# A shorter weight conversion, four more split rows and a reordered plan in a channel-attention kernel

## The chip, the cores and the metric

The kernel runs on one core of a Trainium2 chip. The metric is device time in microseconds, taken as the median of a kernel's runs. The core has four engines that matter here: TensorE (PE, matmuls), VectorE (DVE), ScalarE (ACT) and GpSimd (POOL). SyncE (SP) issues nearly all DMAs. Each engine takes its instructions in the order in which they were written into its queue and waits at an instruction until what it needs is there.

## The reference

Two layers run one after the other on four batches of 6336 rows and 256 channels.

```python
qn = q / (norm(q, axis=1) + 1e-6);  kn = k / (norm(k, axis=1) + 1e-6)
s  = kn.T @ qn / tau                     # 256 x 256 per batch, a sum over 6336 rows
a  = softmax(s);  x = v @ a
gate = sigmoid(sum over 5 taps of conv_w[tap] * x shifted by tap rows)
out  = (gate * (x @ w_val)) @ w_out
```

`q`, `k` and `v` are 32-bit floats. The three weights come as 64-bit floats, because the reference scales them by a 64-bit number. Nothing of `x` is known before a whole batch of `q` and `k` has been summed into `s`, so each batch has two phases: a reduction over rows, then a pass over rows that makes the output.

## The kernel before

**Precision.** A float operand of a matmul is either taken whole (`raw`, 32-bit, slower) or as two halves: a high part rounded to the fast matmul type (ScalarE, line 435) and the rest (GpSimd, line 438). Three fast products, high x high, high x low and low x high, then stand in for one whole product. A "whole row" below is a block of 128 rows whose `q` and `k` go into the matmul as they are; a "split row" is one that goes in as halves.

**Reduction phase.** A batch has 49 blocks of 128 rows and one of 64, in 17 groups: group 0 has one block and the remainder, the others three blocks each. For a group, SyncE loads `q` and `k` (line 412) into one of seven `raw` buffers; ScalarE squares them (462); VectorE or GpSimd adds the squares to one of two running sums (466), whichever the plan picks; TensorE multiplies the rows into `s` (494). `nw` (lines 396 to 399) says how many of a group's blocks stay whole: all three in the first three groups and the last group of batch 0, two in its other groups, two in the first `NATIVE` groups of batch 1, none elsewhere. At the end of a batch the two running sums are added (554), column norms are made on TensorE (544), `s` is copied out of its accumulator (558), scaled, exponentiated, divided (600), transposed (613) and multiplied by `w_val` (626).

**Output phase.** Each batch is passed in 13 steps of 508 rows (the last 240). A step loads `v` (690), transposes (695), casts (699) and splits it (702), makes `x` and `x @ w_val` on TensorE (710), runs the taps mostly on VectorE (736), the sigmoid on ScalarE (747), the product (754), splits it (760, 763) and multiplies it by `w_out` (782), copies (791) and stores (796). The reduction groups of the next batch are put between the steps of this one, so that from the end of batch 0's reduction on both phases run side by side. In the late steps ("shared", `n > LAST_ROWS`) ScalarE and GpSimd take one of VectorE's taps (741, 744), and from a little later on every second step uses two accumulator banks that the reduction no longer needs.

**Weights.** `prepare_weights` turns a 64-bit float, held as a low and an upper 32-bit word, into a 32-bit high part and a low part. It does this with integer operations on VectorE, ten for `w_val` and `w_out` (128 x 512 elements each) and eleven for the small `conv_w`; each operation is a task of its own, so the plan can put other work between them. The scratch tile `f` lies in PSUM, the two words `lo` and `up` in SBUF.

**The plan.** The order of each engine's queue is not written out by hand. Every piece of work is a task with an engine, an estimated cost and its dependencies. `line` fixes a wanted order of TensorE's work; `deadlines` goes back from there and gives every task a due time; `WANTED` gives the weights' loads and conversions theirs. `run` then plays the tasks through in time: an engine takes the task that can start and has the earliest due time. A sum of squares may go to VectorE or GpSimd. A load may start no earlier than `AHEAD` us before it is due. A load is taken to land later by `LAG` (one value early, one late in the kernel, switching at 60 us). `SPREAD` says how many slots after its last group a batch's norms, (batch 0 only) spread, transposes and combine come in `line`. `LATE` sets how many steps ahead of the last batch the groups end. All these figures are the planner's own; they set an order and no time on the chip.

Of the kernel before, what the change touches and what calls it, by code (L numbers as in the profile page):

```python
# [8 lines left out]
F32 = mybir.dt.float32  # L9
# [4 lines left out]
ALU = mybir.AluOpType  # L14
# [2 lines left out]

P = 128
GROUP = 3
LEAD, NATIVE = 4, 4  # L20
VBUFS = 3
Q = 32
SIDE = 3
# [4 lines left out]
class Plan:  # L28
# [65 lines left out]
    def run(self, line):  # L94
        due = self.deadlines(line)
# [21 lines left out]
        dma_free, lanes, table = 0.0, [], "sqrt"  # L117
# [18 lines left out]
        while len(order) < len(T):  # L136
            best = None
            for e, keys in open_.items():
                c = [(r, key) for key in keys for r in [possible(key)] if r is not None]
                if not c:  # L140
                    continue
                now = max(free[e], min(r for r, _ in c))
                if best is None or now < best[0]:
                    best = (now, e, c)
            assert best, "nothing can start"
            now, e, c = best
# [8 lines left out]
            r, key = pick  # L155
            t = T[key]
            start = max(now, r)
            if isinstance(t["cost"], tuple):
                size, n, slow = t["cost"]
                for _ in range(n):  # L160
                    if len(lanes) >= 8:
                        start = max(start, lanes[-8])
                    free[e] = start + SLOT
                    dma_free = max(dma_free, start + SLOT + REACH) + size / n * slow / RATE
                    lanes.append(dma_free)
                    start = free[e]
                end = dma_free + HOP + (LAG[start > 60] if key[0] in "LV" else 0)
            else:
                free[e] = start + self.duration(t, e)
                if t["table"] and t["table"] != table:  # L170
                    table = t["table"]
                    free[e] += TABLE
                end = free[e] + (DRAIN if e == "PE" else HOP if e else 0)
# [33 lines left out]


START, HOP, DRAIN, SLOT, FLIGHT, REACH, RATE = 3.7, 0.12, 0.22, 0.45, 4.5, 1.6, 360000.0
LAG, RAWS = (0.8, 3), 7  # L210
PATIENCE, SLACK, AHEAD = 0.8, 1.5, 26
V_SLOW = 2.0
HEADS = True
NARROW, LATE = (0,), 5
SPREAD = ((0, 0, 0, 0), (3, 3, 3), (1, 2, 1), (0, 1, 0))
TABLE = 1.28
WANTED = {("load", "conv"): 28, ("load", "val"): 15, ("load", "out"): 40, ("ready", "out"): 60, ("ready", "conv"): 32, ("ready", "val"): 38}


@with_exitstack  # L220
def kernel(
# [13 lines left out]
    nc = tc.nc  # L235
# [81 lines left out]
    def prepare_weights(part):  # L317
# [4 lines left out]
        w = parts_w[part]  # L322
        n = w.shape[1]
        if WORDS == 2:
# [4 lines left out]
            yield  # L329
            nc.vector.scalar_tensor_tensor(lo, lo, 17, f, ALU.logical_shift_right, ALU.bitwise_or)  # L330
            yield
            nc.vector.tensor_scalar(f, up, 20, 0x7FF, ALU.logical_shift_right, ALU.bitwise_and)
            yield
            nc.vector.tensor_scalar(f, f, 896.0, 0.0, ALU.subtract, ALU.max)
            yield
            nc.vector.tensor_scalar(f, f, 255.0, 2.0 ** 23, ALU.min, ALU.mult)
            yield
            nc.vector.scalar_tensor_tensor(f, up, -0x80000000, f, ALU.bitwise_and, ALU.bitwise_or)
            yield
            nc.vector.scalar_tensor_tensor(w, lo, 2.0 ** -35, fs, ALU.mult, ALU.mult)  # L340
            yield
            nc.vector.tensor_scalar(f, f, 3, None, ALU.logical_shift_right)
            yield
            nc.vector.scalar_tensor_tensor(f, up, 0xFFE00, f, ALU.bitwise_and, ALU.bitwise_or)
            yield
            nc.vector.tensor_scalar(f, f, 3, None, ALU.logical_shift_left)
            w_high[part] = fs
            if part == "conv":
                yield
# [7 lines left out]
        if WORDS == 2:  # L357
            nc.scalar.copy(flat(halves_w[part][0]), w_high[part])

    PREP = {"val": 10, "conv": 11, "out": 10}  # L360

    def weight_tasks():

# [26 lines left out]
    def group_tasks(b, g):  # L390
# [3 lines left out]
        last = g == len(groups[b]) - 1  # L394
        nv = 2
        if b == 0:
            nw = GROUP if g < SIDE or last else 2
        else:
            nw = 2 if b == 1 and g < NATIVE else 0
        parts = [(P, 0, n)] + [(REST, n, 1)] * rest  # L400
# [557 lines left out]
```

## Time and profile before

| | us |
|---|---|
| runs shown: median (lowest to highest of 3) | 591.97 (591.7 to 593.29) |
| the profiled execution, its own time | 593.26 |
| its span, first to last instruction | 591.5 |
| TensorE busy | 585.7 |
| VectorE busy | 514.3 |
| GpSimd busy | 506.3 |
| ScalarE busy | 479.6 |

The profile is of one execution. A row of a timeline gives start and length in us from the start of the span, engine, source line, operation, the tile written and those read, their shapes, and how many instructions were merged into the row; a bracket at its end gives the idle time of the engine just before and what ended it. Matmuls overlap, so the length of one says little; the distance between starts says what TensorE needs. In a row of grouped instructions the figures behind the bar are busy us, mean ns of one, and idle time before them with what ended it. In the table by stage each engine has its busy time in the stretch, with the number of instructions in brackets, and then the granted TensorE clock, the busy share of the DMA engines and the GB/s moved. SPq and ACTq are the DMA issues on the queues of SyncE and ScalarE.

### The profile page before, as it was taken

To read this page: it belongs to the slowest core of one execution; us is meant where nothing else is said; L and a number is where in the kernel's file an instruction comes from. 1 tells how busy PE (TensorE), PEld (TensorE's weight loads), DVE (VectorE), ACT (ScalarE), POOL (GpSimd) and SP (SyncE) were. 2 spreads that over 40 slices of the span, in tenths; PEclk is the share of its full clock that TensorE was granted. 3 is DMA by queue.
4 is the path that set the end of the run, shared out by engine and by line. 5 is a ranking of instruction groups with operands and counts; after the bars stand their busy time and mean duration, and the time that the engine had idled before them with its cause. 6 is when DMAs were issued, how large, how long until landed. Compare 5 with 4: busy or idle time off the path is not lost.

```text
span 591.5 us, 10511 instructions
## 1 busy us (share of the span) xinstructions
PE 585.7 (99%) x3667; PEld 531.2 (90%) x3667; DVE 514.3 (87%) x792; ACT 479.6 (81%) x582; POOL 506.3 (86%) x241
## 2 busy tenths in 40 slices
PE   9999999999999999999999999999999999999997
PEld 8898899998989999998989998998998998888887
DVE  3996899999989899988788899988969989988774
ACT  6698989889899979787798989788559777767754
POOL 4997999999997999999887999999935778777743
PEclk9999999999999999999999999999999999999999
DMA  8999997958577797874766899678333464553214
GB/s 331 383 368 231 273 243 200 213 133 226 169 157 179 203 214 195 169 190 112 219 166 153 208 213 244 143 190 181 75 93 103 114 160 118 124 141 89 68 40 123
DMA packets 154943, 105.83 MB, mean 179 GB/s; under 512 B 111114, under 2 KB 137994, under 8 KB 154890
## 3 DMA queue, kind: packets, MB, share of 16 engines
q1 hardware_dynamic: 154467, 104.51, 68.7%
q8 instruction: 29, 0.48, 0.4%
q10 hardware_dynamic: 423, 0.65, 0.3%
q14 instruction: 24, 0.20, 0.1%
HBM read 79.18 MB, written 25.95 MB: 178 GB/s over the span
## 4 chain that ended last, share of the span: by engine, by line
PE 89%; DMA 6%; ACT 1%; POOL 1%; issue 1%; SPq 1%; DVE 0%; POOLq 0%; ACTq 0%
PE o_ps L782 24%; PE x_ps L710 23%; PE val_ps L710 23%; PE s_ps L494 17%; DMA raw<-in_q_dram 4%; PE o_ps L626 1%; DMA raw<-in_k_dram 1%; DMA v_raw<-in_v_dram 1%; ACT sq L462 1%; SPq L412 1%; PE o_ps L613 0%; POOL v_lo L702 0%; ACT hi L435 0%; POOL acc L466 0%; PE o_ps L546 0%
## 5 line engine op out<-in xcount | busy, mean ns | idle before, releaser
L736 DVE SCALAR_TENSOR_TENSOR gate<-x_ps,wa,gate 128x508 f32<-128x508 f32 (+1 forms) x400 | 271.2, 717 | 33.9 <-ACT gate L733 31.2
L438 POOL TENSOR_TENSOR lo<-raw,hi 128x1536 fp32r<-128x1536 f32 (+2 forms) x65 | 185.4, 2857 | 7.8 <-ACT hi L435 6.0
L702 POOL TENSOR_TENSOR v_lo<-v_raw,v_hi 128x1024 fp32r<-128x1024 f32 (+1 forms) x52 | 124.1, 2387 | 14.6 <-ACT v_hi L699 12.1
L763 POOL TENSOR_TENSOR g_lo<-gate,g_hi 128x1016 fp32r<-128x1016 f32 (+2 forms) x52 | 120.7, 2322 | 16.9 <-ACT g_hi L760 16.6
L466 DVE TENSOR_TENSOR acc_ps<-acc_ps,sq 128x512 f32<-128x512 f32 (+1 forms) x146 | 101.2, 693 | 21.0 <-ACT sq L462 17.1
L710 PE MATMUL x_ps<-v_hi,w 128*128 128x512 f32 (+2 forms) x416 | 110.1, 384 | 0.0
L710 PE MATMUL val_ps<-v_hi,w 128*128 128x508 f32 (+1 forms) x416 | 107.8, 380 | 0.0
L462 ACT ACTIVATE sq<-raw 128x1536 f32<-128x1536 f32 (+2 forms) x68 | 95.8, 1413 | 3.0 <-POOL acc L466 1.7
L435 ACT CAST hi<-raw 128x1536 fp32r<-128x1536 f32 (+2 forms) x65 | 78.9, 1216 | 19.8 <-PE s_ps L494 11.1
L710 PEld LDWEIGHTS val_ps<-v_hi,w 128*128 128x128 f32 x416 | 76.1, 188 | 14.9
L710 PEld LDWEIGHTS x_ps<-v_hi,w 128*128 128x128 f32 x416 | 72.9, 188 | 12.8 <-POOL w L607 0.4
L733 ACT ACTIVATE gate<-x_ps,wa 128x508 f32<-128x508 f32 (+1 forms) x104 | 68.5, 664 | 14.0 <-PE x_ps L710 13.7
L782 PE MATMUL o_ps<-wo_hi,g_hi 128*127 128x256 f32 (+1 forms) x396 | 79.3, 282 | 0.0
L782 PE MATMUL o_ps<-wo_lo,g_hi 128*127 128x256 f32 (+1 forms) x396 | 79.0, 281 | 0.0
L494 PE MATMUL s_ps<-lo,hi 128*128 128x256 f32 x310 | 78.5, 287 | 0.0
L494 PE MATMUL s_ps<-hi,lo 128*128 128x256 f32 x310 | 77.2, 283 | 0.0
L791 ACT COPY o_sb<-o_ps 127x512 f32<-127x512 f32 (+1 forms) x99 | 57.8, 587 | 23.5 <-PE o_ps L782 23.1
L754 DVE TENSOR_TENSOR gate<-val_ps,gate 128x508 f32<-128x508 f32 (+1 forms) x104 | 67.4, 655 | 4.3 <-ACT gate L747 3.1
L699 ACT CAST v_hi<-v_raw 128x1024 fp32r<-128x1024 f32 (+1 forms) x52 | 57.5, 1107 | 16.0 <-PE val_ps L710 16.0
L466 POOL TENSOR_TENSOR acc<-acc,sq 128x512 f32<-128x512 f32 x46 | 59.9, 1301 | 10.9 <-ACT sq L462 9.6
L747 ACT ACTIVATE gate<-gate 128x1016 f32<-128x1016 f32 (+1 forms) x52 | 53.2, 1022 | 16.2 <-DVE gate L736 15.9
L782 PEld LDWEIGHTS o_ps<-wo_hi,g_hi 128*127 128x127 f32 (+1 forms) x396 | 62.7, 187 | 2.6
(96 smaller groups left out, 948.7 us busy)
## 6 DMA issues: line engine op xcount, KB each, us to landing
raw<-in_q_dram SPq DMA_DIRECT2D x64, 384.0 KB, 5.9
v_raw<-in_v_dram SPq DMA_DIRECT2D x192, 128.0 KB, 5.3
raw<-in_k_dram SPq DMA_DIRECT2D x63, 384.0 KB, 6.2
out_dram<-o_sb SPq DMA_DIRECT2D x47, 448.0 KB, 3.2
out_dram<-o_sb SPq DMA_DIRECT2D x47, 60.0 KB, 3.0
v_raw<-in_v_dram SPq DMA_DIRECT2D x16, 64.0 KB, 2.4
out_dram<-o_sb SPq DMA_DIRECT2D x3, 240.0 KB, 2.7
raw<-in_q_dram SPq DMA_DIRECT2D x4, 128.0 KB, 4.0
```

The costliest lines, as they stand in the source:

```text
L435: nc.scalar.copy(t["hi"][r, js], t["raw"][r, js, :, :])
L438: nc.gpsimd.tensor_tensor(t["lo"][r, js], t["raw"][r, js, :, :], t["hi"][r, js].bitcast(F32), ALU.subtract)
L462: nc.scalar.activation(t["sq"][0:np_, ja:jb], t["raw"][0:np_, ja:jb], AF.Square)
L466: eng.tensor_tensor(st[key][0:np_], st[key][0:np_], t["sq"][0:np_, j], ALU.add)
L494: nc.tensor.matmul(st["s"][:, h, :], lhs, rhs, start="open" not in st, stop=stop)
L702: nc.gpsimd.tensor_tensor(t["vl"][:, :, 0:g, :], t["v"], t["vh"][:, :, 0:g, :].bitcast(F32), ALU.subtract)
L710: nc.tensor.matmul(dst, weights[b][:, which, ws, ch, hs], vs[:, ch, at + lo:at + hi_], start=n_ == 0, stop=n_ == len(ops) - 1)
L733: nc.scalar.activation(t["gate"][:, h, 0:w], t["x", h][:, 0:w], AF.Copy, scale=cw[:, h, 0:1])
L736: nc.vector.scalar_tensor_tensor(t["gate"][:, h, 0:w], t["x", h][:, k_:k_ + w], cw[:, h, k_:k_ + 1], t["gate"][:, h, 0:w], ALU.mult, ALU.add)
L754: nc.vector.tensor_tensor(t["gate"][:, h, 0:w], t["val", h][:, 0:w], t["gate"][:, h, 0:w], ALU.mult)
L763: eng.tensor_tensor(t["gl"][:, hs, 0:w], t["gate"][:, hs, 0:w], t["gh"][:, hs, 0:w].bitcast(F32), ALU.subtract)
L782: nc.tensor.matmul(t["o", p][0:rows, u * C:(u + 1) * C], gs[:, h, j * rows:(j + 1) * rows], ws[:, h, :], start=(u, n_) == (0, 0) if HEADS ...
```

## The change

It has four parts.

- **Conversion.** The exponent and the top 11 bits of the fraction are now taken out of `up` together (shift by 9, mask of 22 bits), and the two clamps run on this longer number. That makes the high part at once; three operations that put the fraction in afterwards fall away. One new operation masks the sign and exponent out of the result into `up`, and the low part is the product of `lo` and `up`, both in SBUF, where it was the product of `lo` and the scratch tile in PSUM. Eight operations are left for the large weights and nine for the small one.
- **Rows.** In groups 3, 6, 9 and 12 of batch 0 (`EASED`) one block stays whole and two are split; it was two and one. `NATIVE` goes from 4 to 5: in group 4 of batch 1 two blocks of three stay whole, where none did.
- **Planner's figures.** `LAG` is now (0.8, 2.5), switching at 30 us (`LAG_AT`); `AHEAD` is 18 for 26; the weights' due times in `WANTED` are changed; and GpSimd may take a sum of squares no earlier than `SPARE` = 100 us before it is due.
- **Order.** `SPREAD` is changed for batches 1 to 3; `LATE` is 4 for 5, so the last group comes one step later, and the shared steps and those with the two extra banks begin one step later.

```diff
-LEAD, NATIVE = 4, 4
+LEAD, NATIVE = 4, 5
...
-                c = [(r, key) for key in keys for r in [possible(key)] if r is not None]
+                c = [(max(r, due[key] - SPARE) if e == "POOL" and key[0] == "A" else r, key) for key in keys for r in [possible(key)] if r is not None]
...
-                end = dma_free + HOP + (LAG[start > 60] if key[0] in "LV" else 0)
+                end = dma_free + HOP + (LAG[start > LAG_AT] if key[0] in "LV" else 0)
...
-LAG, RAWS = (0.8, 3), 7
-PATIENCE, SLACK, AHEAD = 0.8, 1.5, 26
+LAG, RAWS = (0.8, 2.5), 7
+PATIENCE, SLACK, AHEAD = 0.8, 1.5, 18
...
-NARROW, LATE = (0,), 5
-SPREAD = ((0, 0, 0, 0), (3, 3, 3), (1, 2, 1), (0, 1, 0))
+NARROW, LATE = (0,), 4
+SPREAD = ((0, 0, 0, 0), (2, 1, 1), (2, 1, 2), (2, 0, 0))
+SPARE, LAG_AT = 100, 30
+EASED = (3, 6, 9, 12)
...
-WANTED = {("load", "conv"): 28, ("load", "val"): 15, ("load", "out"): 40, ("ready", "out"): 60, ("ready", "conv"): 32, ("ready", "val"): 38}
+WANTED = {("load", "conv"): 28, ("load", "val"): 17, ("load", "out"): 36, ("ready", "out"): 56, ("ready", "conv"): 36, ("ready", "val"): 42}
...
-            nc.vector.tensor_scalar(f, up, 20, 0x7FF, ALU.logical_shift_right, ALU.bitwise_and)
+            nc.vector.tensor_scalar(f, up, 9, 0x3FFFFF, ALU.logical_shift_right, ALU.bitwise_and)
             yield
-            nc.vector.tensor_scalar(f, f, 896.0, 0.0, ALU.subtract, ALU.max)
+            nc.vector.tensor_scalar(f, f, 896.0 * 2 ** 11, 0.0, ALU.subtract, ALU.max)
             yield
-            nc.vector.tensor_scalar(f, f, 255.0, 2.0 ** 23, ALU.min, ALU.mult)
+            nc.vector.tensor_scalar(f, f, 255.0 * 2 ** 11, 2.0 ** 12, ALU.min, ALU.mult)
             yield
             nc.vector.scalar_tensor_tensor(f, up, -0x80000000, f, ALU.bitwise_and, ALU.bitwise_or)
             yield
-            nc.vector.scalar_tensor_tensor(w, lo, 2.0 ** -35, fs, ALU.mult, ALU.mult)
+            nc.vector.tensor_scalar(up, f, -0x800000, None, ALU.bitwise_and)
             yield
-            nc.vector.tensor_scalar(f, f, 3, None, ALU.logical_shift_right)
-            yield
-            nc.vector.scalar_tensor_tensor(f, up, 0xFFE00, f, ALU.bitwise_and, ALU.bitwise_or)
-            yield
-            nc.vector.tensor_scalar(f, f, 3, None, ALU.logical_shift_left)
+            nc.vector.scalar_tensor_tensor(w, lo, 2.0 ** -35, up.bitcast(F32), ALU.mult, ALU.mult)
...
-    PREP = {"val": 10, "conv": 11, "out": 10}
+    PREP = {"val": 8, "conv": 9, "out": 8}
...
-            nw = GROUP if g < SIDE or last else 2
+            nw = GROUP if g < SIDE or last else 1 if g in EASED else 2
```

## The prediction

> **What bounds the kernel now.** I read the page's busy shares first, then the table by stage, then what TensorE waited for, and last the instructions in order of time around each wait.
>
> ```profile
> span 591.5 us, 10511 instructions
> PE 585.7 (99%) x3667; PEld 531.2 (90%) x3667; DVE 514.3 (87%) x792; ACT 479.6 (81%) x582; POOL 506.3 (86%) x241
> ```
> ```profile
> core 0: us, PE busy (x) PEld busy (x) DVE busy (x) ACT busy (x) POOL busy (x), PEclk, DMA share, GB/s
> 24.00:36.00 12.00, 11.66 (x66) 10.57 (x65) 11.35 (x22) 10.71 (x12) 11.20 (x10) 1.00 1.03 402
> 36.00:49.00 13.00, 13.00 (x75) 12.07 (x73) 12.20 (x20) 11.21 (x14) 12.47 (x11) 1.00 1.01 285
> 49.00:62.00 13.00, 12.64 (x74) 10.84 (x73) 6.87 (x16) 10.80 (x18) 9.81 (x8) 1.00 1.00 271
> 62.00:160.00 98.00, 98.00 (x620) 88.86 (x619) 95.90 (x140) 87.34 (x95) 97.92 (x39) 1.00 0.83 202
> ...
> 430.00:490.00 60.00, 60.00 (x375) 53.82 (x374) 50.12 (x79) 44.87 (x68) 36.62 (x20) 1.00 0.49 124
> ...
> 60.00:570.00 510.00, 510.00 (x3231) 1.00 0.68 165
> ```
> ```profile
> PE o_ps L613 <- ACT a L600: 0.4, 1, 0.4
> PE s_ps L494 <- DMA raw<-in_k_dram: 0.3, 1, 0.3
> ```
>
> TensorE is busy 510.00 of the 510 us between 60 and 570, at the full clock. Behind the start it waits twice, 0.3 and 0.4 us (0.34 and 0.36 in the rows further down). The end is short too:
>
> ```profile
> 587.25 0.40 PE L782 MATMUL x_ps<-wo_hi,g_lo 128*120 128x256 f32 x2
> ...
> 588.13 0.35 SPq L803 DMA_DIRECT2D out_dram<-o_end  x1
> ```
>
> From the last matmul's end (587.65) to the end of the span are 3.9 us of copy and store, which no part of the change touches. So the time can move in two ways only: by the work given to TensorE, and by waits of TensorE that close or open. The other engines count when they are late for it. GpSimd and VectorE have little room: 97.92 and 95.90 of 98 us in the stage from 62 to 160, 12.47 and 12.20 of 13 from 36 to 49.
>
> **TensorE's own work.** A group of three rows costs by its mix of whole rows (fp32, four instructions each) and split rows (high and low halves, six each):
>
> ```profile
> 35.49 1.89 PE L494 MATMUL s_ps<-raw 128*128 128x256 f32 x8
> ...
> 37.94 1.89 PE L494 MATMUL s_ps<-raw 128*128 128x256 f32 x8
> ```
> ```profile
> 84.80 2.16 PE s_ps L494 x18
> ```
>
> Two whole rows and one split row take 37.94 - 35.49 = 2.45 us; three split rows take 2.16, so 0.72 each. A whole row is (2.45 - 0.72) / 2 = 0.865, that is 0.145 more. The change turns one whole row into a split one in groups 3, 6, 9 and 12 of batch 0: -4 x 0.145 = -0.58 us. `NATIVE` = 5 leaves two rows of group 4 of batch 1 whole: +2 x 0.145 = +0.29. Net -0.29 us. As TensorE is full, this is gained outright if nothing else is late.
>
> **The waits in batch 0.**
>
> ```profile
> 25.17 2.00 PE L494 MATMUL s_ps<-raw 128*128 128x256 f32 x8 [0.34 <-DMA raw<-in_k_dram]
> ...
> 26.82 0.59 PE L494 MATMUL s_ps<-hi 128*128 128x256 f32 x2
> 27.25 0.36 PE L494 MATMUL s_ps<-lo,hi 128*128 128x256 f32 x1
> ...
> 29.35 0.59 PE L494 MATMUL s_ps<-hi 128*128 128x256 f32 x2
> 29.93 0.39 PE L494 MATMUL s_ps<-lo,hi 128*128 128x256 f32 x1
> ```
> ```profile
> 13.22 1.15 SPq L314 DMA_DIRECT2D w_raw<-in_moe_w_out_dram  x1
> ...
> 17.67 0.33 SPq L412 DMA_DIRECT2D raw<-in_k_dram  x1
> ```
>
> Group 8's keys come 0.34 us late, and the low half of the next group comes late behind them: 29.93 - 29.35 is 0.58 where 27.25 - 26.82 is 0.43, so 0.15 more. The 512 KB of w_out stand at 13.22 in SyncE's queue, ahead of groups 7 and 8 (17.67 is group 8's k). Their load is due at 40 now and issued up to `AHEAD` = 26 us early, from 14 on in the planner's own clock; with 36 and 18 it is opened at 18, behind those groups, and a landing 10 us later is covered, as the first out product needs batch 0's softmax, which has reached only its division at 58 (below). At the 402 GB/s of that stage 0.52 MB are 1.3 us, more than the 0.34 needed, even after the 2 x 0.145 by which groups 3 and 6 let TensorE arrive earlier (0.34 + 0.29 = 0.63). w_val's load (due 15, now 17) steps behind group 6 in the same way. Term: -0.34 - 0.15 = -0.49; the bounds are -0.49 and, with loads as late as now and TensorE earlier, +0.58 (the whole saving of batch 0 spent waiting). I take the first, since 1.3 is twice 0.63.
>
> **What the other engines pay.**
>
> ```profile
> L438 POOL TENSOR_TENSOR lo<-raw,hi 128x512 fp32r<-128x512 f32 x18 | 23.1, 1288 | 1.0 <-ACT hi L435 1.0
> L702 POOL TENSOR_TENSOR v_lo<-v_raw,v_hi 128x1024 fp32r<-128x1024 f32 x48 | 118.9, 2476 | 14.3 <-ACT v_hi L699 11.8 <-DMA v_raw<-in_v_dram 2.4
> L466 DVE TENSOR_TENSOR acc_ps<-acc_ps,sq 128x512 f32<-128x512 f32 x142 | 98.4, 693 | 20.3 <-ACT sq L462 16.4
> L342 DVE TENSOR_SCALAR w_ps<-w_ps 128x512 int32<-128x512 int32 x2 | 1.4, 685 | 0.0
> ```
>
> Four second rows cost GpSimd 4 x (2.476 - 1.288) = 4.75 us in batch 0. Two conversion operations less for w_val and w_out save VectorE 4 x 0.685 = 2.74 (those of the ten-column conv weights come on top). The square sums may run on either engine: four sums moved from GpSimd, which takes 1.29 for any two-input operation of this shape, to VectorE give GpSimd 5.2 and cost VectorE 4 x 0.693 = 2.77. So both come out even; VectorE has 0.8 us spare from 36 to 49 besides. ScalarE's four longer casts (1.47 for three rows further down, so at most 0.49 for one more, 2.0 in all) fit in its idle 1.8 us from 36 to 49 and 1.3 from 24 to 36. I take 0 for all this, because the sums are dealt by due time to whichever engine is free. If none moved, GpSimd would be 4.75 late where its margin is small:
>
> ```profile
> 42.24 1.31 POOL L438 TENSOR_TENSOR lo<-raw,hi 128x512 fp32r<-128x512 f32 x1
> ...
> 44.80 0.28 PE L494 MATMUL s_ps<-lo,hi 128*128 128x256 f32 x1
> ```
>
> The low half ends at 43.55 and is used at 44.80: 1.25 us. So TensorE would wait 4.75 - 1.25 = 3.5. In batch 1 `NATIVE` takes two rows off a full GpSimd, about 2.4 us, so no debt is carried on.
>
> The new last conversion step reads both words from SBUF, where the old one read one from PSUM. No row here shows VectorE with two SBUF inputs beside GpSimd. Between 0 and one VectorE step for w_val and w_out each, 2 x 0.685 = 1.4 us of GpSimd, I take 0, as the margin above covers one. The Trainium skill ("SBUF — State Buffer", Who interferes with whom) says that such an instruction takes the read port of GpSimd, and the later of the two is blocked for the whole of the other. By that rule GpSimd loses the 1.4; no run here shows it yet.
>
> **The softmax of batch 0.**
>
> ```profile
> 46.18 0.69 DVE L554 TENSOR_TENSOR acc_all<-acc_ps,acc 128x512 f32<-128x512 f32 x1 [0.29 <-POOL acc L466]
> 48.13 0.59 ACT L558 COPY s<-s_ps 128x512 f32<-128x512 f32 x1
> 48.97 0.97 PE L544 MATMUL o_ps<-ones,acc_all 128*128 128x1 f32 x8
> ...
> 56.70 1.47 ACT L435 CAST hi<-raw 128x1536 fp32r<-128x1536 f32 x1 [1.04 <-POOL v_lo L702]
> 58.08 0.90 ACT L600 ACTIVATE a<-s,rz 128x256 f32<-128x256 f32 x2
> 58.64 0.84 PE L613 MATMUL o_ps<-ident,a 128*128 128x128 f32 x4 [0.36 <-ACT a L600]
> ```
>
> The norms follow the copy of s, which follows batch 0's last row, so this chain starts earlier by what batch 0 gains (its sums are done 1.3 us before the copy). Its one wait, 0.36, comes from a cast that stands ahead of the division on ScalarE and itself waits 1.04 us. The longer load time from 30 us on (`LAG_AT`) may reorder those two. Bounds -0.36 and +1.04 (the same stall twice on the path); I take 0.
>
> **What moves without a price.** `LATE` = 4 lets the groups run one step longer, and one shared step fewer moves 0.7 us from ScalarE and 1.3 from GpSimd to VectorE (0.7), in a stage (430 to 490) where VectorE is 50 of 60 us busy. Batch 3's softmax starts about a step later, some 10 us (the 527 us from 60 to the last matmul over 52 steps). It has that room: from its last row products to the first use of its weights are
>
> ```profile
> 442.69 1.44 PE s_ps L494 x12
> ...
> 478.02 0.62 PE L710 MATMUL x_ps<-v_hi,w 128*128 128x508 f32 x2
> ```
>
> 34 us, and batch 0's softmax took 9.7 from norms to transposes. `SPARE` = 100 bars GpSimd from a sum more than 100 us before it is due; with seven raw buffers none is loaded so early. `SPREAD` moves norms, transposes and combines by one to five slots in the order; TensorE takes the earliest due that can start, so I take 0, between -0.29 and +0.7 for each of three softmaxes: the one is what is lost at such a border now, the other two waits of batch 0's size.
>
> ```profile
> 307.44 0.84 PE L494 MATMUL s_ps<-hi 128*128 128x256 f32 x4
> 308.21 0.39 PE L494 MATMUL s_ps<-lo,hi 128*128 128x256 f32 x1
> ```
>
> Here four instructions take 0.77, where four of 0.72 / 6 = 0.12 take 0.48.
>
> **The sum.** -0.58 + 0.29 - 0.49 = -0.78 us. The profiled execution took 593.26 (span 591.5 and 1.76 around it), so 592.5 of its like; it lies 1.29 above the median of the runs, 591.97, which gives 591.2.
>
> **The rivals.**
>
> - The loads bind batch 0 anyway (1.03 of the DMA engines are busy there): TensorE's 0.58 turns into waiting and only `NATIVE` is left: 591.97 + 0.29 = 592.3. Against it speaks w_out's step back.
> - The waits close everywhere: -0.78, the 0.36, and three times 0.29 at the later softmaxes: -2.0, 590.0. It needs every reordering to hit.
> - Slower: GpSimd becomes the bound of batch 0, as its four longer subtractions stay in front of TensorE and the sums do not move: +3.5 less the 0.29 net saving, 595.2. It decides from the point at which no more than one of the four sums moves: at one, GpSimd is 4.75 - 1.29 - 1.25 = 2.2 late (593.9), at two 0.9 (592.6).
> - The port: 1.4 us of GpSimd fall on TensorE in place of none: 591.2 + 1.4 = 592.6. The skill's rule named above would make this one; the margin of 1.25 speaks against it.
> - Loads opened 18 and not 26 us ahead come late in the later stages. The longest landing up to 60 us (the last figure here) was 9.4 us and the due time already holds a flight of 4.5, so this needs a second cause; waits as long as batch 0's three together (0.34 + 0.36 + 1.04) give 591.2 + 1.7 = 592.9.
>
> ```profile
> DMA to landing us min/median/max: 2.7/6.9/9.4
> ```
>
> **How the numbers follow.** Forecast 0.50 (its own range 590.6 to 591.8), loads bind 0.16, all waits close 0.12, GpSimd binds 0.09, port 0.07, late loads 0.06. A measurement of this kernel tells about 0.3%, 1.8 us, from no change. Faster than 590.2 are most of the all-close case and the edge of the forecast: 0.12. Slower than 593.8 is GpSimd's case and a little of the late loads: 0.10. Within: 0.78. The range 590.0 to 592.9 leaves out GpSimd's case, half of the late loads and part of the fastest.
>
> **What would show it.** Right: eight raw matmuls fewer and twelve split ones more; w_out's load behind group 8's; no wait on a DMA at group 8; the sums of batch 0 with four fewer on GpSimd; norms about 1 us before 48.97; TensorE still full from 60 to 570. Wrong: TensorE waiting for a low half (L438) or raw in the stage 24 to 49, a GpSimd operation beside the new conversion step that is longer than 1.3 us, or new waits at the softmaxes of batches 1 to 3.

## The result and the profile after

The changed kernel takes 597.21 us (median of four executions, 597.12 to 598.37); the kernel before, timed beside it, takes 591.84 (591.62 to 593.29). The ratio is 1.009, with a 95% interval of 1.0078 to 1.0102. The change makes the kernel 5.4 us slower, where 0.8 us less was forecast. The profiled execution took 597.12 us.

The head of the page of the kernel after:

```profile
span 595.3 us, 10546 instructions
PE 587.1 (99%) x3671; PEld 532.0 (89%) x3671; DVE 517.9 (87%) x788; ACT 479.3 (81%) x581; POOL 506.8 (85%) x239
```

TensorE has four matmuls more (eight whole ones fewer, twelve of split rows more), as counted beforehand. The loss is found in the table by stage of the same kernel (the columns are named in its first line):

```profile
core 0: us, PE busy (x) PEld busy (x) DVE busy (x) ACT busy (x) POOL busy (x), PEclk, DMA share, GB/s
24.00:36.00 12.00, 11.73 (x70) 10.67 (x69) 10.98 (x22) 11.13 (x12) 9.76 (x7) 1.00 1.03 404
36.00:49.00 13.00, 12.21 (x69) 10.97 (x67) 12.44 (x18) 8.88 (x11) 9.33 (x8) 1.00 1.10 296
49.00:62.00 13.00, 12.19 (x62) 10.96 (x62) 12.55 (x20) 9.17 (x18) 7.78 (x6) 0.87 1.15 280
62.00:160.00 98.00, 96.72 (x607) 87.14 (x607) 93.74 (x137) 87.12 (x95) 96.56 (x40) 1.00 0.81 181
...
160.00:570.00 410.00, 410.00 (x2602) 371.68 (x2601) 360.29 (x543) 333.04 (x411) 359.23 (x161) 1.00 0.65 159
```

From 160 to 570 TensorE is full, as before. What is lost is lost ahead of 66 us (from 62 to 66 TensorE is busy for 2.72 of 4 us, from 66 to 160 for all 94): from 49 to 62 it starts 62 matmuls where the kernel before started 74, and its clock is 0.87. GpSimd, taken beforehand for the engine that could become late, is less busy there than before (9.33 for 12.47 us from 36 to 49, 7.78 for 9.81 from 49 to 62). VectorE is the fuller one from 49 to 62: 12.55 us for 6.87, and 4.10 of the 12.55 are one operation that comes below.

The view of what TensorE waited for, kernel after (total us, times, longest):

```profile
PE o_ps L542 <- DVE acc_all L552: 1.6, 1, 1.6
...
PE o_ps L624 <- ACT at_hi L615: 1.1, 1, 1.1
PE s_ps L492 <- DMA raw<-in_k_dram: 0.2, 1, 0.2
```

The two new waits are for the sums of batch 0 (line 552) and for its transposed weights (line 615), both parts of the softmax of batch 0; the 0.2 us for keys lie at 5.70, at the start. The same two places on TensorE's timeline, with the first matmul that uses the weights (line 708), which started at 60.04 before:

```profile
49.81 1.08 PE L542 MATMUL o_ps<-ones,acc_all 128*128 128x1 f32 x8 [1.60 <-DVE acc_all L552]
...
63.14 0.74 PE L624 MATMUL o_ps<-wv_hi,at_hi 128*128 128x256 f32 x4 [1.10 <-ACT at_hi L615]
...
64.66 0.62 PE L708 MATMUL x_ps<-v_hi,w 128*128 128x508 f32 x2
```

Why they are late is on VectorE's timeline. Line 344 is the new last step of the conversion, the one with both inputs in SBUF; `wa` are the conv weights, `wv_lo` and `wo_lo` the low parts of w_val and w_out; line 552 adds the two running sums; line 580 is the softmax's scale:

```profile
28.34 0.72 DVE L344 SCALAR_TENSOR_TENSOR wa<-w_raw 128x10 f32<-128x10 int32 x1
...
38.70 1.71 DVE L344 SCALAR_TENSOR_TENSOR wv_lo<-w_raw 128x512 fp32r<-128x512 int32 x1
...
49.06 0.69 DVE L552 TENSOR_TENSOR acc_all<-acc_ps,acc 128x512 f32<-128x512 f32 x1
...
51.87 4.10 DVE L344 SCALAR_TENSOR_TENSOR wo_lo<-w_raw 128x512 fp32r<-128x512 int32 x1
...
56.50 0.86 DVE L580 SCALAR_TENSOR_TENSOR s<-s,nk,o_ps 128x256 f32<-128x256 f32 x2
```

An operation of this shape took 0.685 us before. Here w_val's step takes 1.71 and w_out's 4.10, and even the ten columns of the conv weights take 0.72. GpSimd beside the two long ones:

```profile
39.82 1.73 POOL L464 TENSOR_TENSOR acc<-acc,sq 128x512 f32<-128x512 f32 x1
...
51.69 1.28 POOL L464 TENSOR_TENSOR acc<-acc,sq 64x512 f32<-64x512 f32 x1 [1.21 <-ACT acc L455]
52.92 1.27 POOL L436 TENSOR_TENSOR lo<-raw,hi 128x512 fp32r<-128x512 f32 x1
54.15 1.27 POOL L464 TENSOR_TENSOR acc<-acc,sq 128x512 f32<-128x512 f32 x1
55.63 1.48 POOL L464 TENSOR_TENSOR acc<-acc,sq 128x512 f32<-128x512 f32 x1 [0.20 <-ACT sq L460]
```

w_out's step starts 0.18 us after a GpSimd operation did. Three GpSimd operations then keep their length, 1.27 or 1.28. GpSimd has nothing to do from 55.42 to 55.63; w_out's step ends at 55.97, and the GpSimd operation behind that pause takes 1.48. w_val's step got in at the next change of operations: it ends at 40.41, and the GpSimd operation that started at 39.82 takes 1.73 in place of 1.29.

### The profile page after: what moved, and what is told of

Its sections match the earlier page's. It is cut to its first block, busy times and chain, and to the rows that moved or that the text cites. A ratio compares the mean times of both kernels' runs of the same rounds, so it can differ in the third digit from the quotient of the medians.

```text
span 595.3 us, 10546 instructions
## 1 busy us (share of the span) xinstructions
PE 587.1 (99%) x3671; PEld 532.0 (89%) x3671; DVE 517.9 (87%) x788; ACT 479.3 (81%) x581; POOL 506.8 (85%) x239
## 4 chain that ended last, share of the span: by engine, by line
PE 89%; DVE 5%; issue 2%; DMA 2%; ACT 2%; POOL 1%; SPq 0%; DVEq 0%; ACTq 0%; POOLq 0%
PE o_ps L780 24%; PE x_ps L708 23%; PE val_ps L708 23%; PE s_ps L492 17%; DVE acc_ps L464 3%; DMA raw<-in_k_dram 2%; ACT sq L460 1%; PE o_ps L624 1%; POOL lo L436 0%; ACT hi L433 0%; PE o_ps L542 0%; POOL acc L464 0%; DVE wv_lo L344 0%; PE o_ps L544 0%; PE o_ps L611 0%
## 5 line engine op out<-in xcount | busy, mean ns | idle before, releaser
L436 POOL TENSOR_TENSOR lo<-raw,hi 128x1536 fp32r<-128x1536 f32 (+3 forms) x65 | 186.4, 2874 | 10.9 <-ACT hi L433 10.8
L433 ACT CAST hi<-raw 128x1536 fp32r<-128x1536 f32 (+3 forms) x65 | 79.5, 1227 | 7.0 <-DMA raw<-in_k_dram 4.1
L464 POOL TENSOR_TENSOR acc<-acc,sq 128x512 f32<-128x512 f32 (+1 forms) x45 | 58.8, 1306 | 9.2 <-ACT sq L460 7.3
L780 PE MATMUL o_ps<-wo_hi,g_lo 128*127 128x256 f32 (+1 forms) x396 | 63.3, 282 | 0.0
```

The source lines that it names most:

```text
L433: nc.scalar.copy(t["hi"][r, js], t["raw"][r, js, :, :])
L436: nc.gpsimd.tensor_tensor(t["lo"][r, js], t["raw"][r, js, :, :], t["hi"][r, js].bitcast(F32), ALU.subtract)
L464: eng.tensor_tensor(st[key][0:np_], st[key][0:np_], t["sq"][0:np_, j], ALU.add)
L780: nc.tensor.matmul(t["o", p][0:rows, u * C:(u + 1) * C], gs[:, h, j * rows:(j + 1) * rows], ws[:, h, :], start=(u, n_) == (0, 0) if HEADS ...
```

## The experiments

Two theories stood at the start: the new last step loses time to GpSimd, since both its inputs are in SBUF (the port); or the new figures of the planner and the rows give a worse order (the order).

**The changed kernel without the second SBUF input (a_psum).** The three steps swap their scratch tiles, so that the eight operations stay and the last one reads one input from PSUM. The order of the work stays the same.

```diff
-            nc.vector.scalar_tensor_tensor(f, up, -0x80000000, f, ALU.bitwise_and, ALU.bitwise_or)
+            nc.vector.scalar_tensor_tensor(up, up, -0x80000000, f, ALU.bitwise_and, ALU.bitwise_or)
...
-            nc.vector.tensor_scalar(up, f, -0x800000, None, ALU.bitwise_and)
+            nc.vector.tensor_scalar(f, up, -0x800000, None, ALU.bitwise_and)
...
-            nc.vector.scalar_tensor_tensor(w, lo, 2.0 ** -35, up.bitcast(F32), ALU.mult, ALU.mult)
-            w_high[part] = fs
+            nc.vector.scalar_tensor_tensor(fs if part == "conv" else w, lo, 2.0 ** -35, fs, ALU.mult, ALU.mult)
+            w_high[part] = up.bitcast(F32)
```

(`up` is in SBUF; `f` and `fs` are the scratch tile in PSUM. The sum of the two parts of the conv weights follows suit.)

> The changed kernel with its eight conversion operations, their order and every other instruction's place as they are; only the last steps use other operands: the merged high part goes to the SBUF word, the masked sign and exponent to PSUM, so that the low part is made from one SBUF and one PSUM input. Theory (port): the low-part operation with two SBUF inputs waits on VectorE until GpSimd pauses (0.72, 1.71 and 4.10 us instead of 0.16 and 0.68); without it all three are back at 0.16 to 0.7, the softmax of batch 0 is 3.4 us earlier, and the time falls to 592 to 593.5. Rival (plan): the queues' new order is what makes the sums late; it is the same here, so the time stays at 596 to 597.5.

593.07 us (592.58 to 594.7), ratio to before 1.0021 [1.0011, 1.0031], as the port had it. So 4.1 of the 5.4 us go away with this one input. What is left is 1.2 us by the ratio, and 0.9 between the medians timed side by side (before 592.15). The three steps in the view by source line (ns, minimum/median/maximum), and the same places as above on the timeline:

```profile
L344 DVE SCALAR_TENSOR_TENSOR w_ps<-w_raw,w_ps x1: 161/161/161, 28.2 to 28.2; 128x10 f32<-128x10 int32 x1
L344 DVE SCALAR_TENSOR_TENSOR wv_lo<-w_raw,w_ps x1: 676/676/676, 38.0 to 38.0; 128x512 fp32r<-128x512 int32 x1
L344 DVE SCALAR_TENSOR_TENSOR wo_lo<-w_raw,w_ps x1: 678/678/678, 50.1 to 50.1; 128x512 fp32r<-128x512 int32 x1
```
```profile
47.30 0.69 DVE L552 TENSOR_TENSOR acc_all<-acc_ps,acc 128x512 f32<-128x512 f32 x1
...
48.04 1.08 PE L542 MATMUL o_ps<-ones,acc_all 128*128 128x1 f32 x8
...
51.59 0.87 DVE L580 SCALAR_TENSOR_TENSOR s<-s,nk,o_ps 128x256 f32<-128x256 f32 x2 [0.20 <-PE o_ps L548]
...
60.31 0.62 PE L708 MATMUL x_ps<-v_hi,w 128*128 128x508 f32 x2
```

The port's price in the changed kernel can be followed along this chain: the two early steps lose 0.56 + 1.04 = 1.6 us on VectorE, the sums are 1.76 later, the norms 1.77, the scale 4.91, the first use of the weights 4.35, the end of the span 4.5 (595.3 and 590.8). The sums of a_psum end at 47.99 and its norms start at 48.04, so a stall ahead of the sums has no room there.

**The old conversion under the new figures (a_oldconv)**, and **the new conversion alone in the kernel before, with one PSUM input (b_psum) and with two SBUF inputs (b_newconv)**. In all three the planner lays out the order anew for the number of operations.

```diff
 a_oldconv, in the kernel after:
-    PREP = {"val": 8, "conv": 9, "out": 8}
+    PREP = {"val": 10, "conv": 11, "out": 10}
 (and the ten conversion lines of before)
 b_newconv and b_psum, in the kernel before:
-    PREP = {"val": 10, "conv": 11, "out": 10}
+    PREP = {"val": 8, "conv": 9, "out": 8}
 (and the eight conversion lines, as after or as in a_psum)
```

> The changed kernel with the old conversion of ten operations put back; the plan orders the queues anew around it, with the changed due times, rows and figures. Theory (port): no operation reads two SBUF inputs, so 592 to 593.5. Rival (plan or rows): VectorE has 2.7 us more to do under the same due times, so 597 or more.

> The kernel before with only the new conversion of eight operations. Theory (port): its low-part operations stall behind GpSimd as in the changed kernel, 1 to 4 us each, and the softmax of batch 0 or the sums come late: 593.5 to 596. Rival (plan): two operations fewer with the old order of the rest, 591 to 592.

> The kernel before with the eight operations in the form that reads one SBUF and one PSUM input. Theory (port): no stall, 591 to 592, the same as before. Rival (eight operations in themselves upset the plan): as slow as the kernel before with the two-SBUF form.

a_oldconv: 597.45 us, 1.0084 [1.0067, 1.0101]. b_newconv: 615.85, 1.0399 [1.0383, 1.0414]. b_psum: 615.35, 1.0388 [1.0372, 1.0403]. All three lie outside the range of the port; a_oldconv and b_psum came out as the rival, the plan, had it. These two are slow without any such stall on the large weights: b_psum's large steps take 679 and 680 ns, a_oldconv's 678 and 692 (b_newconv's take 1511 and 1579). Most of the loss lies far from the conversion, that of a_oldconv too, which takes as long as the changed kernel but waits elsewhere. What TensorE waited for in b_psum, then in a_oldconv:

```profile
PE x_ps L706 <- DVE gate L732: 6.9, 2, 4.1
PE x_ps L706 <- DVE x_ps L712: 6.5, 1, 6.5
```
```profile
PE x_ps L712 <- DVE gate L738: 2.7, 2, 2.3
```

These are waits in the late steps, after 430 us. So an order laid out anew can cost 23 us without any port, and these runs can't price the conversion. What follows is that edits have to be compared in a fixed order.

**The kernel before, profiled a second time (before_again).**

> The kernel before once more, for a second profile: the profiled execution of before took 593.26 us where the median is 592. If the 0.34 us that TensorE waited for the keys of group 8 and the 0.15 behind it are part of every execution, they stand here too at the same place; if they belong to the slower execution alone, a profile near 591.7 us does not have them, and the term of -0.49 us in the prediction was never there to gain.

592.67 us, span 590.9. TensorE waits for the zeros at the start (1.2 us) and for nothing else: neither the 0.34 us at group 8 nor the 0.36 at the transposes is there, with the same instructions.

**The new conversion in the order of before (b_keep_sb, b_keep_psum).** The eight operations are put into the kernel before, and `PREP` stays at 10/11/10, so that the planner lays out the old order and two of the ten places stay empty. b_keep_sb has two SBUF inputs, b_keep_psum one of each kind.

```diff
     PREP = {"val": 10, "conv": 11, "out": 10}
-(ten conversion lines)
+(eight conversion lines, as after or as in a_psum)
```

> The kernel before with the new conversion, in the queues' order of before: the plan still counts ten and eleven conversion tasks, of which the last two emit nothing. So the order is that of before, two operations are gone, and the low part reads two SBUF inputs. Theory (port): the low-part operations for w_val and w_out wait for pauses of GpSimd, as they did in the changed kernel, for 0.5 to 3 us each, and the kernel takes 592.5 to 596. Rival (only the order hurts): 591.5 to 592.5.

> The same order of before, the eight operations in the form with one SBUF and one PSUM input. Both theories: no stall, 591.5 to 592.5. If it were as slow as the kernel with eight operations that the plan ordered anew (615), the operations and not the order would be at fault there.

b_keep_sb: 592.23 us, 1.0006 [0.9997, 1.0015]. b_keep_psum: 591.9, 0.9999 [0.999, 1.0009]. b_keep_sb has the stall and doesn't pay for it. Its timeline of VectorE:

```profile
42.58 2.34 DVE L342 SCALAR_TENSOR_TENSOR wo_lo<-w_raw 128x512 fp32r<-128x512 int32 x1
...
46.36 0.69 DVE L550 TENSOR_TENSOR acc_all<-acc_ps,acc 128x512 f32<-128x512 f32 x1
```

There w_out's step stands ahead of the last sums, and these are still added where they were (46.36; 46.18 before); they end at 47.05, 1.7 us ahead of the norms (48.75). w_val's step has no stall there (678 ns). So the stall costs only where something that TensorE needs soon stands behind it. And two operations fewer per weight are worth nothing that can be measured in this order.

**The port by itself (probe_sb, probe_ps).** The kernel before gets one extra VectorE multiplication of 128x508 in each of 19 steps, whose result nobody reads: once with both inputs in SBUF, once with one in PSUM.

```diff
+            if h == 1 and 14 <= n < 34 and w == ROWS:
+                nc.vector.tensor_tensor(t["val", h][:, 0:w], t["gate"][:, 0, 0:w], t["gate"][:, 1, 0:w], ALU.mult)
 (probe_ps: the first input is t["val", h][:, 0:w], in PSUM)
```

> The kernel before with one more VectorE multiplication of 128 x 508 per output step in steps 14 to 33 (18 of them), both inputs in SBUF, the result into the step's value bank in PSUM, which nobody reads again. GpSimd is 98% busy in these steps. Theory (port): each takes 0.68 us plus a wait for a pause of GpSimd, so between 1 and 8 us, and GpSimd's next operation starts late; the kernel is slower by several us. Rival (a plain VectorE operation): 0.65 to 0.75 us each, the kernel within 2 us of before.

> The same multiplications at the same places, but the first input is the PSUM bank itself, so one input is in SBUF and one in PSUM. Both theories: 0.65 to 0.75 us each and the kernel within 2 us of before; it is the control for the other probe.

probe_sb: 619.27 us, 1.0459 [1.0424, 1.0494]. probe_ps: 593.16, 1.0018 [1.0007, 1.003]. The 19 operations by source line, in probe_sb and then in probe_ps:

```profile
L756 DVE TENSOR_TENSOR val_ps<-gate x19: 695/915/10682, 229.6 to 468.5; 128x508 f32<-128x508 f32 x19
```
```profile
L756 DVE TENSOR_TENSOR val_ps<-val_ps,gate x19: 695/695/696, 230.3 to 443.5; 128x508 f32<-128x508 f32 x19
```

The longest one on VectorE's timeline, and GpSimd's timeline around it, both of probe_sb:

```profile
229.57 10.68 DVE L756 TENSOR_TENSOR val_ps<-gate 128x508 f32<-128x508 f32 x1
```
```profile
227.99 2.45 POOL L702 TENSOR_TENSOR v_lo<-v_raw,v_hi 128x1024 fp32r<-128x1024 f32 x1
230.41 3.52 POOL L438 TENSOR_TENSOR lo<-raw,hi 128x1536 fp32r<-128x1536 f32 x1
233.89 2.40 POOL L765 TENSOR_TENSOR g_lo<-gate,g_hi 128x1016 fp32r<-128x1016 f32 x1
236.26 3.43 POOL L438 TENSOR_TENSOR lo<-raw,hi 128x1536 fp32r<-128x1536 f32 x1
247.68 2.42 POOL L702 TENSOR_TENSOR v_lo<-v_raw,v_hi 128x1024 fp32r<-128x1024 f32 x1 [7.99 <-ACT v_hi L699]
```

VectorE's operation starts within the first of four GpSimd operations that follow each other without a pause, stands through the other three too, and ends at 240.25, 0.56 after the last of them (239.69). With an input in PSUM the same multiplication takes 0.695 us every time (696 ns at most). That settles the port for the operation itself.

**The port-free kernel with other figures of the planner (a_psum_six), and once more as it was (a_psum_again).**

```diff
 a_psum_six, against a_psum:
-PATIENCE, SLACK, AHEAD = 0.8, 1.5, 18
+PATIENCE, SLACK, AHEAD = 0.8, 1.5, 22
-NARROW, LATE = (0,), 4
-SPREAD = ((0, 0, 0, 0), (2, 1, 1), (2, 1, 2), (2, 0, 0))
-EASED = (3, 6, 9, 12)
+NARROW, LATE = (0,), 3
+SPREAD = ((0, 0, 0, 0), (2, 1, 1), (2, 3, 0), (2, 0, 0))
+EASED = (4, 8, 9, 12, 14, 15)
 (and in WANTED w_out's load due at 40, not 36)
```

> The changed kernel with the low part made from one SBUF and one PSUM input, and other figures for the plan: six groups of batch 0 with one whole row (4, 8, 9, 12, 14, 15), AHEAD 22, LATE 3, SPREAD (2, 3, 0) for batch 2, w_out's load due at 40. Two whole rows fewer are 2 x 0.145 = 0.29 us less for TensorE than in the changed kernel. If TensorE stays full, 592.0 to 593.0, about 0.3 below the form with four rows; if the extra low halves make GpSimd late in batch 0, 593.5 to 596.

> The changed kernel with one SBUF and one PSUM input once more, for a second profile: its profiled execution was the shortest of ten (592.58, median 593.07) and lay level with the second profile of before. If some executions have waits on loads that others lack, they show here; if the two profiles agree within 0.3 us in every stage, the 0.9 us between the medians stays unexplained by waits of TensorE.

a_psum_six: 591.62 us (591.32 to 592.07), 0.9991 [0.9982, 1.0]; it is the fastest version, below its expected range and at the very edge of what can be told from the kernel before. So rows and order can be had at no loss. As the eight operations cost nothing in the old order (b_keep_psum), the 1.2 us that a_psum keeps over the kernel before are put down to its rows and its order; which of them, these runs don't tell. a_psum_again's profiled execution took 593.23, with one wait of 0.4 us behind a cast (line 433) that the first profile of the same kernel hasn't. Three of a_psum's ten executions ran at a mean clock of 0.997 and took 594.5 to 594.7, the other seven at 1.0 and took 592.6 to 593.2.

**One half of the port's stalls at a time (a_out_psum, a_early_psum).** In the kernel after, the port-free form is given to w_out alone (the early stalls are left), or to w_val and the conv weights alone (w_out's stall is left).

```diff
-            w_high[part] = fs
+            w_high[part] = up.bitcast(F32) if part == "out" else fs
 (the three other swapped lines likewise; a_early_psum: part != "out")
```

> The changed kernel in its own order, where only w_out's low part is made from one SBUF and one PSUM input; w_val's and the conv weights' are left with two SBUF inputs. It splits the loss of 4.1 us in two. Theory: w_val and conv stall (1.0 and 0.6 us) ahead of the sums of batch 0, so that the norms come late, TensorE waits 1.6 us and its clock drops; w_out's stall (3.4 us) stands in front of the softmax's scaling, and TensorE waits about 1.1 us more. With w_out's stall gone the norms' wait and the clock drop stay, and the time is 595 to 596.5. Rival: w_out's stall alone carries the loss, 592.6 to 593.6.

> The complement of the kernel where only w_out's low part was mended: w_val's and the conv weights' low parts are made from one SBUF and one PSUM input, w_out's is left with two SBUF inputs. Theory: the sums and the norms are on time, TensorE does not wait for them and its clock stays full; w_out's stall (up to 3.5 us in front of the softmax's scaling) is left, and TensorE waits about 1 to 2.5 us for it: 593.5 to 595.5. Rival: any one stall is enough for the whole loss, 596.5 to 597.5.

a_out_psum: 596.96 us, 1.0073 [1.0054, 1.0093]. a_early_psum: 595.71, 1.0067 [1.0052, 1.0082]. Both lie a little above the range of the theory. Against a_psum's 593.07 the early stalls alone cost 3.9, w_out's alone 2.6, both together 4.1: each is more than half of the whole. One line of VectorE's timeline of a_early_psum shows the stall that is left there; the other three are of a_out_psum (TensorE's norms and their broadcast, then VectorE's scale):

```profile
50.45 4.10 DVE L344 SCALAR_TENSOR_TENSOR wo_lo<-w_raw 128x512 fp32r<-128x512 int32 x1
```
```profile
50.31 1.17 PE L542 MATMUL o_ps<-ones,acc_all 128*128 128x1 f32 x8 [1.58 <-DVE acc_all L552]
...
54.87 1.05 PE L548 MATMUL o_ps<-ident,rq 128*128 128x128 f32 x4
```
```profile
55.96 0.88 DVE L580 SCALAR_TENSOR_TENSOR s<-s,nk,o_ps 128x256 f32<-128x256 f32 x2 [2.20 <-PE o_ps L548]
```

In a_out_psum the scale has no stall ahead of it, and waits 2.20 us for TensorE all the same: for the broadcast of the norms (line 548), which TensorE reaches late. This profile is of the slowest of the four executions (598.08).

**A filled gap ahead of the norms (a_fill, a_fill_data, a_out_fill).** Behind the wait for the sums TensorE's granted clock is halved; the clock column (the figure behind the number of instructions) of the table by stage of the kernel after, where 51 to 52 has 0.96:

```profile
52.00:53.00 1.00, 1.00 (x5) 0.50 1.55 188
...
54.00:55.00 1.00, 1.00 (x4) 0.50 1.09 291
55.00:56.00 1.00, 1.00 (x5) 0.83 1.05 363
```

The theory was that this makes up part of the early stalls' price. Ten matmuls whose results the norms overwrite fill the wait: of zeros in a_fill, of w_val's high half in a_fill_data; a_out_fill is a_out_psum with the latter.

```diff
+            for _ in range(10 if b == 0 else 0):
+                nc.tensor.matmul(t["n"][:, 0:C], wv_hi[:, 0, 0:P], wv_hi[:, 0, :], start=True, stop=True)
 (a_fill: zeros for both)
```

> The changed kernel with ten matmuls of zeros (128 x 256, about 0.12 us each) put on TensorE just ahead of batch 0's norms, into the norms' own bank, which the norms then overwrite. They need the bank but not the sums, so they run in the time in which TensorE waited for the sums. Theory (clock): TensorE is idle for less than 0.6 us there and keeps its full clock, so the 3.3 us at half clock behind the wait (1.65 us lost) are gone: 595 to 596. Rival (only the waits count): 597 to 598, as the filler adds what it does not hide.

> The changed kernel with the ten filler matmuls ahead of batch 0's norms made from w_val's high half, 128 x 256, in place of zeros. Theory (activity): matmuls of zeros do not count as work for the clock, those of data do; the clock stays at 1.00 and the time is 595 to 596. Rival (the wait of some 0.4 us and the norms of one column behind it are enough): the clock halves for 3.3 us as it did with zeros, and the time is 597 to 597.8.

> The kernel after, with w_out's low part made from one SBUF and one PSUM input (so only the two early port stalls are left), and ten products of w_val's high half put ahead of batch 0's norms, whose results the norms overwrite. Without the ten products this kernel had a wait of 1.6 us for acc_all, then TensorE at half clock from 51.4 to 58, and the softmax's scale on VectorE (line 580 there) waited 2.20 us for the broadcast of the norms on TensorE (line 548), at 55.96; 596.96 us. Theory A (clock): where the w_out stall is gone, the scale hangs on TensorE, and the half clock between the norms and their broadcast is what puts it late. With the gap filled the clock stays up, the broadcast starts some 1.9 us behind the norms' end and not 3.4, the scale comes at about 54 us, and the time falls by about 1.5 to 2 us, to 595 to 595.5. Theory B (sums alone): the late sums put everything late, whatever the clock; the time stays at 596.5 to 597.4.

a_fill: 597.42 us, 1.0091 [1.0074, 1.0108]; its profile still has the half clock, so the zeros didn't keep the clock up there. a_fill_data: 597.58, 1.0094 [1.0077, 1.0111]; its profile has 1.00 throughout, and it is no faster. So in the changed kernel the half clock costs nothing that shows, and the theory fell. a_out_fill: 594.56, 1.0043 [1.0027, 1.006], which is 2.4 less than a_out_psum, more than was expected. Without w_out's stall the clock does count. The same three places in a_out_fill (TensorE's timeline, then VectorE's):

```profile
49.61 1.08 PE L544 MATMUL o_ps<-ones,acc_all 128*128 128x1 f32 x8 [0.41 <-DVE acc_all L554]
...
52.51 0.60 PE L550 MATMUL o_ps<-ident,rq 128*128 128x128 f32 x4
```
```profile
53.16 0.87 DVE L582 SCALAR_TENSOR_TENSOR s<-s,nk,o_ps 128x256 f32<-128x256 f32 x2 [0.20 <-PE o_ps L550]
```

From the norms to the broadcast it takes 52.51 - 49.61 = 2.9 us, where a_out_psum took 54.87 - 50.31 = 4.56 for the same matmuls. The 0.7 by which the norms themselves start earlier in a_out_fill isn't the clock's: the sums come that much earlier there, ahead of the filled gap (line 554 starts at 48.86, line 552 of a_out_psum at 49.57). The executions agree on the direction: a_out_psum took 597.6 and 598.1 at a mean clock of 0.994, 596.2 and 596.35 at 0.997, and a_out_fill 594.2 to 594.8 at 1.0. Against the two at 0.997 the gain is 1.7, not 2.4.

So the scale is reached on two ways, and the later one counts: through VectorE, behind w_out's stall, and through TensorE, behind the late sums and the half clock. That fits two prices that don't add. Of the early stalls' 3.9 us, 2.4 go with the filled gap by the medians (596.96 - 594.56; 1.7 against the executions at 0.997), and 1.5 are left (594.56 - 593.07), with the sums still late.

## Why the prediction was wrong, point by point

**TensorE's own work (-0.29)** held in its counts (3671 matmuls for 3667). TensorE was to be full from 60 to 570 and was busy for 508.72 of the 510 us; the rest, 1.28, is the wait for the transposed weights and one of 0.18 us, both between 62 and 66. The size of the term is too small for these runs' times to show.

**The waits in batch 0 (-0.49).** w_out's load went where it was foreseen, to 28.38 in SyncE's queue, behind the loads of group 8:

```profile
28.38 0.38 SPq L316 DMA_DIRECT2D w_raw<-in_moe_w_out_dram  x1
```

But the term was worth nothing. The wait it was to close was that of one execution; before_again hasn't got it. A single profile was taken for the kernel's state, although its 593.26 us already lay 1.3 above the median.

**What the other engines pay (0).** The dealing of the sums held. By source line up to 49 us GpSimd has 17 of them before and 10 after; VectorE has 34 and 38, so three fewer fall into this stretch in all:

```profile
L466 POOL TENSOR_TENSOR acc<-acc,sq x17: 1269/1288/1317, 7.3 to 47.8; 128x512 f32<-128x512 f32 x17
```
```profile
L464 POOL TENSOR_TENSOR acc<-acc,sq x10: 1272/1286/1733, 7.3 to 44.3; 128x512 f32<-128x512 f32 x10
```

The case of GpSimd as the bound (595.2) is the one whose time lies nearest to the result, yet its mechanism wasn't seen: GpSimd has more idle time than before.

**The port (0, bounds 0 and 1.4): here the prediction failed**, in the step "Between 0 and one VectorE step for w_val and w_out each, 2 x 0.685 = 1.4 us of GpSimd, I take 0, as the margin above covers one." Three things in it were wrong.

- Who pays. The 1.4 were charged to GpSimd. GpSimd lost 0.44 us beside w_val's step (1.73 for 1.29) and 0.20 beside w_out's (1.48 for 1.28); the engine that waited is VectorE.
- How much. The three steps lost 0.56 + 1.04 + 3.42 = 5.0 us of VectorE in place of at most 1.4, since the bound took a collision to last as long as one step. w_val's lasted until the next change of GpSimd operations, w_out's until GpSimd paused, three operations later.
- What stands behind it. The margin of 1.25 us was that of GpSimd's low halves. What queues behind a stalled VectorE is the sums of batch 0 and the scale of its softmax, and the prediction's bounds on that softmax (-0.36 and +1.04) were drawn from ScalarE's casts alone.

The rival of the port (592.6) had the right place and the right sign, with the price of the wrong engine. The Trainium skill ("SBUF — State Buffer", Who interferes with whom) has it that a VectorE instruction with two SBUF inputs contends with a GpSimd instruction that reads SBUF, that the one issued first keeps the shared port for the whole instruction, and that the other is blocked outright. By that the loser depends on the order of issue, and the prediction had worked out only the case in which it is GpSimd. The runs agree on the pair (with one input in PSUM the multiplication took 0.695 us every time) and on the blocking, whose loser in the changed kernel is VectorE above all (5.0 us; GpSimd 0.64 in the two rows named). They go further in one point: the block outlasted not one GpSimd instruction but four in a row, 10.68 us.

**The softmax of batch 0 (0).** "Starts earlier by what batch 0 gains" holds without the port: in a_psum the norms start at 48.04, 0.93 before the 48.97 of before, where about 1 was foreseen. Luck has a part in the number: in before_again, which hasn't the wait at group 8, they start at 48.78, so 0.74 are left. In the changed kernel they start 0.84 later. The chain was read wrongly, too. The norms don't follow the copy of `s`, which starts at 48.04 in the changed kernel (48.13 before); they follow the sums. Those had 2.1 us to spare before (46.87 to 48.97) and in a_psum, where VectorE has taken more of them, 0.05 (47.99 to 48.04). So the new plan had used up the room before the port took 1.6 us more, and the prediction put no price on that.

**What moves without a price (0).** The late loads, the later batches and the steps from 430 on showed no wait of TensorE in the changed kernel. Yet a_psum keeps 1.2 us over the kernel before, where the forecast's terms give a gain: even without the port the time, 593.07, is just above the range's 592.9. a_psum_six shows that other figures take the 1.2 back. Which row or figure it is stays open. That the order cost no more than this was luck rather than knowledge: with the old conversion under the same figures (a_oldconv) and the new one under the old figures (b_psum) it cost 5.3 and 23, against the kernel before timed beside them.

Of the 5.4 us, then, 4.1 are the port's, shown by the exchange of one input in an unchanged order, and 1.2 come with rows and order, by what is left over.

## What to carry to other kernels

Beside a GpSimd that works without a pause, give each VectorE instruction with two tensor inputs one of them in PSUM where that is possible. Where both must be in SBUF, allow for a wait until GpSimd next pauses, and look at what stands behind it on VectorE, for a stall with nothing urgent behind it is free (2.34 us for w_out's step, 592.23 us in all) and a stall in front of a softmax that TensorE waits for is not. Before a wait in a profile is booked as a gain, look whether a second profile of the same kernel has it. And where a planner lays out the order, compare an edit in the old order first: eight operations for ten cost 23 us re-planned and nothing in the order as it was.

## What the runs showed of the hardware that was not expected

- A VectorE operation with two SBUF inputs doesn't get in between two GpSimd operations reliably: w_val's did at the first change (1.71 us), w_out's stood through three such operations (4.10), the probe's through four (10.68). What decides it isn't known.
- A wait of TensorE of 1.6 us was followed by half clock, from 51.9 to 55.3 in the kernel after and from 51.1 to 58.0 in a_out_psum, so about 3.4 us and twice that. By the mean clock of the executions, 0.003 less goes with some 1.5 us more where TensorE's way is the later one (a_out_psum, a_psum; no profile shows where a_psum's slower executions lost their clock) and with nothing where it isn't (a_fill, 597.42 at 0.997 and 597.44 at 1.0). The Trainium skill ("TensorE: Matmul & The Clock Gate", What's actually happening) puts the half clock behind at least one idle window of about 3.4 us, and the return behind a busy one as long. The half clock of the kernel after agrees in length with one such window; the wait ahead of it, 1.6 us, was half of that.
- Zeros in the gap left the half clock in the one profile of a_fill; a matrix of data left none in those of a_fill_data and a_out_fill. But a_fill had a full clock in two other executions and a_fill_data had 0.996 and 0.997 in three, so whether the data matter stays open.
